# Attention backward on one core: V's fourth head is loaded as 120 rows and 8 rows, in two transfers

## The chip, the core and the metric

The kernel runs on one NeuronCore of a Trainium2 chip. The metric is device microseconds (us) of one execution. The kernel before was run three times: 698.41, 701.58 and 702.56 us, so its median is 701.58 us. The profile is of a further execution, which took 698.71 us.

## The reference

The kernel computes grouped-query softmax attention and all its gradients, in bfloat16. There are 32 batches, 32 query heads of 4 positions, 4 key/value heads of 2048 positions, and a head dimension of 128.

```python
k = jnp.repeat(k, 8, axis=1); v = jnp.repeat(v, 8, axis=1)     # 4 heads -> 32
scores = jnp.einsum("bhqd,bhkd->bhqk", q, k) * D ** -0.5
out = jnp.einsum("bhqk,bhkd->bhqd", softmax(scores), v)
dq, dk, dv = vjp(grad_out)                                     # four outputs: out, dq, dk, dv
```

K and V are read once (2 MB of each per batch), dK and dV are written once (2 MB of each per batch); q, grad_out, out and dq are small beside them (32 KB each per batch). So each batch moves a little over 8 MB between HBM and the on-chip memory SBUF.

## The kernel before

The work goes batch by batch. One batch has 128 query rows in all (32 heads x 4 positions), which fill the 128 partitions. A key/value head of 2048 positions lies in SBUF as 128 partitions (p) x 16 positions (c) x 128 elements, so that one partition's piece of one head is 4096 contiguous bytes in HBM.

For each batch the kernel loads K (`LK`, line 154, one transfer of 128 rows x 4096 bytes for each of four heads) and V (`LV`, line 160, likewise four). TensorE turns K and V, eight blocks of 128x128 at a time (`turned`, L181), and VectorE copies each result out of PSUM (L183). Then come scores (L198), maximum (L211), exponential on ScalarE (L222), the turned probabilities (L248, L250), the output `O` (L264, L274), the gradients of V (`dV`, L303 on TensorE, copied by ScalarE at L307), the gradient of the scores (`dP`, L338), its turned form, dQ (L264, L288) and dK (again L303 and L307). GpSimd scales the small operands of dV and dK (L231, in `NRM`).

What sets the order is a list of steps written out by hand, one list for the first batches (`HEAD`), one for the steady state (`STEADY`), one for the last (`TAIL`). Every engine executes its instructions in that order. In the steady state the loads of a batch (`LK+2 LV+2`) stand two batches ahead of the rest of the work, and the transposes of K and V one batch ahead.

Two queues issue transfers. SyncE (SP) issues all loads of K and V, in the order k0 k1 k2 k3 v0 v1 v2 v3 for each batch (the digit is the head). GpSimd (POOL) issues everything else: the stores of dV and dK (L326, two of 1 MB each per batch and gradient), of out (L276) and dq (L290), and once in four batches a load of q and grad_out (L142). Both queues feed the same 16 DMA engines. In the trace every transfer writes its completion semaphore 16 times, once for each DMA engine, so the time at which each of the 16 was done can be read, though not which engine it was. A 4096-byte row is one packet, and a load of 128 rows puts eight packets on each engine.

Three limits decide when a transfer can be issued:

- Its buffer must be free. K has three buffers (`kp`), V two (`vp`), the gradients on their way out four (`outp`), which is two batches of dV and dK.
- Its completion semaphore must be free. Each queue has eight of them (100 to 105, 107 and 109 for SP) and takes them in turn, so a transfer waits until the one that was issued eight before it on the same queue has landed.
- A queue issues in order, so a transfer that waits holds up all behind it.

Of the kernel before, what the change touches and what calls it, by code (L numbers as in the profile page):

```python
# [81 lines left out]
def kernel(ctx: ExitStack, tc: tile.TileContext, q, k, v, grad_out, out_0, out_1, out_2, out_3):  # L82
    nc = tc.nc
    B, Hq, Sq, D = q.shape
    NH, Sk = k.shape[1], k.shape[2]
    P = 128
# [41 lines left out]
    v_v = v.rearrange("b h (p c) d -> b h p (c d)", c=C)  # L128
# [27 lines left out]
    def LV(b):  # L156
        S = st[b]
        S["v"] = v_pool.tile([P, NH, C, D], BF16, name="v_sb")
        for h in range(NH):
            nc.sync.dma_start(out=S["v"][:, h].rearrange("p c d -> p (c d)"), in_=v_v[b, h])  # L160

    def bank16():

# [170 lines left out]
    def dP(b, i):  # L334
# [6 lines left out]
        banks.give(t)  # L341

    table = {"LK": LK, "LV": LV, "QDT": QDT, "O": O, "dQ": dQ, "NRM": NRM}
    for i, c in enumerate("ab"):
        for n, f in (("S", S_), ("EX", EX), ("dP", dP), ("ET", ET), ("dST", dST)):
# [16 lines left out]
    with tc.manual_schedule():  # L362

        for w in HEAD.split():
            w, b = w.split("@")
# [5 lines left out]
        for w in TAIL.split():  # L371
            w, b = w.split("@")
# [31 lines left out]
```

## Time and profile before

| | |
|---|---|
| profiled execution | 698.71 us, of which 696.7 us lie between the first and the last instruction (the span) |
| granted TensorE clock | 0.980 over the span |
| PE (TensorE) busy | 626.0 us, 90% of the span |
| DVE (VectorE) busy | 584.5 us, 84% |
| ACT (ScalarE) busy | 569.1 us, 82% |
| POOL (GpSimd) busy | 302.7 us, 43% |
| moved by DMA | 274.44 MB, mean 394 GB/s |
| issue to landing, median | k 13.8 us, v 18.6 us, dv 23.6 us, dk 22.1 us |

The page gives for each engine how long it was busy, then the span in 40 equal slices, in which a digit is the busy share in tenths. The DMA row is the mean over 16 engines. "Landing" is the last of the 16 completions of a transfer. The chain of waits is followed back from the last instruction: at each step to whatever released it. A line like "DMA out_dram<-dk" in it means that the time went by between the issue of that transfer and its landing, while something waited for it.

### The profile page before, as it was taken

To read this page: it belongs to the slowest core of one execution; us is meant where nothing else is said; L and a number is where in the kernel's file an instruction comes from. 1 tells how busy PE (TensorE), PEld (TensorE's weight loads), DVE (VectorE), ACT (ScalarE), POOL (GpSimd) and SP (SyncE) were. 2 spreads that over 40 slices of the span, in tenths; PEclk is the share of its full clock that TensorE was granted. 3 is DMA by queue.
4 is the path that set the end of the run, shared out by engine and by line. 5 is a ranking of instruction groups with operands and counts; after the bars stand their busy time and mean duration, and the time that the engine had idled before them with its cause. 6 is when DMAs were issued, how large, how long until landed. Compare 5 with 4: busy or idle time off the path is not lost.

```text
span 696.7 us, 28064 instructions
## 1 busy us (share of the span) xinstructions
PE 626.0 (90%) x12352; PEld 454.1 (65%) x12352; DVE 584.5 (84%) x992; ACT 569.1 (82%) x673; POOL 302.7 (43%) x506
## 2 busy tenths in 40 slices
PE   5899999999998989979999798998998889998982
PEld 4577776677676656666666676667766677666661
DVE  5999999999997998869988688888988869898960
ACT  0698989899887989869888687887888868888994
POOL 1355443555454435443354424544434543345452
PEclk9999999999999999999999899999999989999997
DMA  9989999999999999999999999999999999999767
GB/s 339 400 317 411 417 415 416 416 413 415 417 415 417 414 417 416 417 409 412 415 415 413 373 397 398 400 410 382 416 416 417 415 340 393 415 414 415 289 257 274
DMA packets 75577, 274.44 MB, mean 394 GB/s; under 512 B 8448, under 2 KB 8448, under 8 KB 75456
## 3 DMA queue, kind: packets, MB, share of 16 engines
q0 software_dynamic: 37536, 138.16, 49.3%
q1 hardware_dynamic: 37920, 134.50, 48.9%
q8 instruction: 96, 1.57, 0.8%
q14 instruction: 25, 0.20, 0.1%
HBM read 136.31 MB, written 136.31 MB: 391 GB/s over the span
## 4 chain that ended last, share of the span: by engine, by line
PE 43%; DMA 33%; ACT 6%; DVE 5%; POOL 5%; issue 5%; SPq 0%; POOLq 0%; DVEq 0%; ACTq 0%
PE banks L181 18%; DMA k_sb<-in_k_dram 15%; DMA out_dram<-dk 12%; PE banks L303 10%; PE banks L264 7%; ACT dv L307 5%; PE banks L248 5%; DMA out_dram<-dv 4%; PE banks L198 3%; POOL dop L231 2%; DMA v_sb<-in_v_dram 2%; DVE kt L183 2%; DVE ds L338 1%; ACT dk L307 1%; POOL qp L231 1%
## 5 line engine op out<-in xcount | busy, mean ns | idle before, releaser
L307 ACT CAST dv<-banks 128x1024 bf16<-128x1024 f32 x256 | 245.5, 1028 | 56.9 <-PE banks L303 56.3
L307 ACT CAST dk<-banks 128x1024 bf16<-128x1024 f32 x256 | 250.7, 1025 | 34.5 <-PE banks L303 23.6
L183 DVE COPY kt<-banks 128x1024 bf16<-128x1024 bf16 x256 | 164.3, 680 | 8.3 <-PE banks L181 8.3
L183 DVE COPY vt<-banks 128x1024 bf16<-128x1024 bf16 x256 | 166.2, 680 | 1.3 <-PE banks L181 0.9
L181 PE MATMUL banks<-ident,k_sb 128*128 128x128 bf16 x2048 | 145.8, 221 | 13.1 <-DMA k_sb<-in_k_dram 8.6
L181 PE MATMUL banks<-ident,v_sb 128*128 128x128 bf16 x2048 | 143.5, 220 | 14.3 <-ACT dv L307 9.7
L231 POOL TENSOR_SCALAR dop<-do_sb,rinv 32x128 bf16<-32x128 bf16 x128 | 76.7, 599 | 181.3 <-PE banks L303 118.9
L181 PEld LDWEIGHTS <-k_sb 128*128 128x128 bf16 x2048 | 120.8, 99 | 41.9 <-issue 31.7
L181 PEld LDWEIGHTS <-v_sb 128*128 128x128 bf16 x2048 | 122.2, 98 | 28.7 <-issue 23.3
L303 PE MATMUL banks<-dop,e 64*128 64x256 bf16 x1024 | 99.3, 276 | 15.1 <-POOL dop L231 11.3
L326 POOL DMA_DIRECT2D out_dram<-dv x62 | 43.7, 709 | 138.0 <-ACT dv L307 67.6
L338 DVE SCALAR_TENSOR_TENSOR ds<-banks,delta,e 128x1024 bf16<-128x1024 f32 x64 | 82.2, 1284 | 17.3 <-PE banks L198 14.3
L303 PE MATMUL banks<-qp,ds 64*128 64x256 bf16 x1024 | 86.4, 272 | 2.1 <-ACT dk L307 1.4
L231 POOL TENSOR_SCALAR qp<-q_sb,srinv 32x128 bf16<-32x128 bf16 x128 | 78.1, 610 | 10.7
L222 ACT ACTIVATE e<-banks,negb 128x1024 bf16<-128x1024 f32 x64 | 70.7, 1111 | 8.6 <-DVE negb L214 8.5
L211 DVE TENSOR_REDUCE m<-banks 128x1 f32<-128x1024 f32 x64 | 75.1, 1215 | 0.9 <-PE banks L198 0.9
L303 PEld LDWEIGHTS <-e 64*128 64x128 bf16 x1024 | 34.0, 94 | 63.1 <-issue 46.7
L250 DVE COPY et<-banks 128x1024 bf16<-128x1024 bf16 x64 | 41.3, 686 | 29.6 <-PE banks L248 29.6
L303 PEld LDWEIGHTS <-ds 64*128 64x128 bf16 x1024 | 42.2, 94 | 28.8 <-ACT dv L307 13.1
L326 POOL DMA_DIRECT2D out_dram<-dk x62 | 44.0, 713 | 13.6 <-DMA out_dram<-dk 13.0
L250 DVE COPY dst<-banks 128x1024 bf16<-128x1024 bf16 x64 | 43.5, 681 | 5.5 <-PE banks L248 3.6
L248 PE MATMUL banks<-ident,ds 128*128 128x128 bf16 x512 | 39.4, 221 | 7.1 <-ACT dk L307 6.8
(39 smaller groups left out, 484.1 us busy)
## 6 DMA issues: line engine op xcount, KB each, us to landing
k_sb<-in_k_dram SPq DMA_DIRECT2D x128, 512.0 KB, 13.8
v_sb<-in_v_dram SPq DMA_DIRECT2D x128, 512.0 KB, 18.6
out_dram<-dv POOLq DMA_DIRECT2D x64, 1024.0 KB, 23.6
out_dram<-dk POOLq DMA_DIRECT2D x64, 1024.0 KB, 22.1
out_dram<-o_sb POOLq DMA_DIRECT2D x32, 32.0 KB, 23.2
out_dram<-dq_sb POOLq DMA_DIRECT2D x32, 32.0 KB, 16.2
q_sb<-in_q_dram POOLq DMA_DIRECT2D x7, 128.0 KB, 21.9
do_sb<-in_grad_out_dram POOLq DMA_DIRECT2D x7, 128.0 KB, 22.0
```

What stands on the lines that cost most here:

```text
L181: nc.tensor.transpose(out=ps[:, 4 * hh + j, :], in_=S[which][:, 2 * (i % 2) + hh, 4 * (i // 2) + j, :], identity=ident[:])
L183: nc.vector.tensor_copy(out=S[f"{which}t{i}"][:], in_=ps)
L211: nc.vector.reduce_max(out=S["m"][:, i:i + 1], in_=S[f"s{i}"][1], axis=AX.X)
L222: nc.scalar.activation(out=S[f"e{i}"][:], in_=ps, func=ACT.Exp, bias=S["negb"][:], scale=scale, accum_out=S["l"][:, i:i + 1],)
L231: nc.gpsimd.tensor_scalar(out=t[r, h % 2, :], in0=src[r, :], scalar1=by[r, :], scalar2=None, op0=ALU.mult)
L248: nc.tensor.transpose(out=ps[:, u, :], in_=S[f"{src}{i}"][:, P * u:P * u + P], identity=ident[:])
L250: nc.vector.tensor_copy(out=S[f"{name}{i}"][:], in_=ps)
L264: nc.tensor.matmul(ps[G * h:G * h + G, :], lhsT=S[f"{xt}{c // 8}"][:, c % 8, G * h:G * h + G], rhs=S[kv][:, h, c, :], start=(c == 0), stop ...
L303: nc.tensor.matmul(ps[:, a, :, c, :], lhsT=S[f"{x}{i // 4}"][r, u:u + P], rhs=S[y][r, :, :], start=True, stop=True, tile_position=(2 * G * ...
L307: copy(out=S[name][:, :, 2 * i:2 * i + 2, :].rearrange("p h c d -> p h (c d)"), in_=banks.ap(t).rearrange("p a (j w) -> p (a j) w", j=2),)
L326: store.dma_start(out=dst[b][:, 2 * a:2 * a + 2, :], in_=o[:, 2 * a:2 * a + 2].rearrange("p h c d -> p h (c d)"))
L338: nc.vector.scalar_tensor_tensor(out=S[f"ds{i}"][:], in0=ps, scalar=S["delta"][:], in1=S[f"e{i}"][:], op0=ALU.subtract, op1=ALU.mult,)
```

## The change

The loads of V's heads 0 to 2 stay as they are. The load of head 3 becomes two transfers on the same queue: rows 0 to 119 (480 KB), then rows 120 to 127 (32 KB). They write the same bytes of the same buffer.

```diff
         for h in range(NH):
-            nc.sync.dma_start(out=S["v"][:, h].rearrange("p c d -> p (c d)"), in_=v_v[b, h])
+
+            for r in (slice(0, 120), slice(120, P)) if h == NH - 1 else (slice(0, P),):
+                nc.sync.dma_start(out=S["v"][r, h].rearrange("p c d -> p (c d)"), in_=v_v[b, h, r])
```

In the program built from it SP has 32 more transfers, one for each batch, and TensorE 32 more waits on a semaphore, because a reader of V's fourth head waits for both transfers. Nothing else moves: TensorE, VectorE, ScalarE and GpSimd execute the same instructions in the same order. The eight completion semaphores of the queue are still taken in turn, now by nine transfers for each batch. So each transfer waits on a different one than before: the third head of V on the 120 rows of the batch before, the 120 rows on the 8 rows of the batch before, and the 8 rows on the first head of K of their own batch.

## The prediction

> **What bounds the kernel now.** I read the DMA rows first: the page's slices and queues, then the busy time by stage (after the colon-marked stage and its length: TensorE, its weight loads, VectorE, ScalarE, GpSimd, then clock, DMA share and GB/s). DMA is full from 4 to 650 us; TensorE has some 8% to spare after 180 us.
>
> ```profile
> DMA  9989999999999999999999999999999999999767
> ...
> q8 instruction: 96, 1.57, 0.8%
> ```
> ```profile
> 60.00:180.00 120.00, 117.22 (x2366) 85.56 (x2355) 110.31 (x190) 108.33 (x130) 56.62 (x94) 1.00 1.03 415
> 180.00:380.00 200.00, 183.61 (x3656) 131.66 (x3657) 172.99 (x293) 168.20 (x199) 91.19 (x151) 0.99 1.03 414
> 380.00:640.00 260.00, 237.53 (x4642) 172.09 (x4636) 219.61 (x374) 213.63 (x254) 113.20 (x186) 0.97 1.01 400
> ```
>
> Until 180 us TensorE is busy 117.22 of 120 us and batches follow each other every 19.5 us (in the chain of waits the copies of dv come at 128.43, 147.92 and 167.44 us). From 180 us on the chain of waits is made of transfers: first loads of K, once per batch and 21.1 us apart, later stores waited for by ScalarE because all four output buffers are out.
>
> ```profile
> 199.11 16.95 DMA k_sb<-in_k_dram
> ...
> 220.24 16.81 DMA k_sb<-in_k_dram
> ...
> 241.24 17.01 DMA k_sb<-in_k_dram
> ...
> 615.44 27.13 DMA out_dram<-dk
> 642.67 1.02 ACT dk L307
> ```
>
> A transfer ends with the last of its 16 engines. I took the 16 completion times of each transfer from the trace; medians from issue, us:
>
> | stage | transfers | 1st | 8th | 15th | 16th |
> |---|---|---|---|---|---|
> | 60–180 | loads | 9.6 | 11.7 | 12.9 | 14.6 |
> | 180–380 | loads | 6.9 | 12.8 | 14.6 | 19.9 |
> | 380–640 | loads | 5.5 | 6.6 | 8.4 | 15.1 |
> | 380–640 | stores of dk, dv | 8.9 | 9.3 | 10.8 | 23.9 |
>
> So **one engine is late in every transfer**: the store issued at 615.44 us was done on 15 engines at 627.98 us and on the sixteenth at 642.57 us. For each place in the order I subtracted from the time the work done by then (155.4 ns per 4096-byte packet, the distance from start to start on a busy engine; 80 ns per 2048-byte packet; 6 ns per semaphore write). What is left, at 80, 380 and 640 us: the first 11.4, 13.2, 30.4 us; the eighth to fifteenth about 12.7, 20.8, 32; **the sixteenth 12.7, 28.3, 44.3**. The last loses 31.6 us in 560 us, 5.64%, and never rests: in the trace its packets run alone from 653.9 to 657.2 us. Followed packet by packet back from 655 to 460 us they take 167.8 ns on average, where the median of all packets is 159. The middle eight lose 8.1 us from 80 to 380 us, 2.7%; the 96 instruction packets of queue q8, each of which I see delay one engine by about 1.27 us, would cost eight engines 15.2 us each over the run, 2.6%. After 380 us the fifteen wait for the one: their own losses of 11 us more are idle time, in bursts.
>
> **The change, part by part.**
>
> *What an engine has to do.* Per batch: 128 packets x 155.4 = 19.89 us, plus two 2048-byte packets, one packet of q or grad_out and some 14.5 semaphore writes, 0.40: **20.29 us**. With its loss the late engine needs 20.29 / (1 - 0.0564) = **21.50 us**, a middle one 20.29 / (1 - 0.027) = 20.85.
>
> *The 120 rows.* How they spread the trace doesn't show. The nearest row is the 128-row load with eight packets on each of 16 engines. Bounds: each engine keeps eight rows, so fifteen engines work and one has none (15 x 8 = 120); or all sixteen still take part with seven or eight, and none is relieved. I take the first, since it is the existing division with one share missing. The missing share is the last in order; I take the late engine to be at the end, since in stores of the tail (issued at 657.26 us) the other fifteen completed at even steps of 13 to 20 ns with no hole before the last, where a late engine in the middle would leave one. That is a weak sign, and the first rival is built on it. Relief: 8 x 163.8 (167.8 less 4 overlap) = 1.31 us per batch, which leaves the late engine at 20.19 us.
>
> *The 8 rows.* Bounds: one packet more on eight engines (+0.16 us with the semaphore write) or eight on one (+1.25 us). I take one packet each, by the same row, where each engine has an equal share, and put them on the middle eight, the worse place: 20.85 + 0.16 = **21.01 us**. That is then the slowest engine.
>
> The Trainium skill (DMA: Bandwidth & Descriptors, "Why a DMA increments its semaphore by 16 and not by 1") says the number of engines is the largest divisor of the row count up to 16, the lowest-numbered ones on this queue: fifteen for 120, eight for 8. By that rule, which no run here shows yet, the sum is the one taken.
>
> *The issue.* 32 more issues on SP at 0.33 to 0.47 us, in a queue that stands waiting for buffers and landings:
>
> ```profile
> SPq L154 <- PE banks L303: 293.5, 29, 13.4
> SPq L160 <- PE banks L303: 80.2, 27, 5.1
> SPq L160 <- DMA v_sb<-in_v_dram: 72.3, 46, 2.5
> ...
> SPq L154 <- DMA k_sb<-in_k_dram: 52.0, 33, 2.4
> ```
>
> Cost nothing: 293.5 us of waiting for buffers cover 32 x 0.47 = 15 us. Without that cover it would be 0.5 us per batch.
>
> *The waits.* Nine transfers share eight semaphores, so v2 and the 120 rows wait for a landing one transfer later than now, and the 8 rows for k0 of their own batch; behind them in SP stand the next batch's four K loads. k0 has landed 13.8 us after its issue (median), while v3 is issued some 12 us after k0: about 2 us later than now, and k0 of the next batch comes 9 us after that. Of loads in flight seven large ones are left, 56 packets per engine, and with the stores taking turns 56 x 2 x 155 ns = 17.4 us of queue, still full. I take zero; the bounds are a gain of nothing and the third rival's loss. TensorE's extra wait per batch: a semaphore wait of 17 ns on SP and POOL, 32 x 17 ns = 0.5 us, left out.
>
> *Sum.* 21.50 - 21.01 = 0.49 us per batch. From 180 to 657 us the DMA sets the pace: 477 / 21.5 = 22.2 batches, **10.9 us**. Taking off 1.4 us for pauses that don't come from the late engine (TensorE waits 4.1 us for "issue" at 389 and 562 us, and the DMA runs dry around them) leaves 9.5. The tail after 657 us has 39 us in which the DMA isn't full; I leave it as it is. What is late next are the middle eight engines. 698.71 - 9.5 = 689.2 us against the profiled execution. The median of the runs stands 2.9 us above that execution, so the same gain gives 692.1 there; midway between the two I predict **690.5**. Something under 1%, 7 us, is what a measurement of this kernel can tell from no change.
>
> **The rivals.**
>
> *Another engine is the late one.* Then it isn't relieved, and if it is among the eight it gets a row more: 21.50 + 0.16 us over 22.2 batches, +3.6 us, up to 32 x 0.16 = +5.2: 702 to 707. For: no view gives the engine's number. Against: the even steps above. The Trainium skill (same page, "Latency and other measured facts") calls engines 7 and 15 usually slower, and guesses that descriptors of the GpSimd queue are the cause. The trace agrees in part: in the opening, with loads alone, eight loads in a row end with the same 0.80 us between the fifteenth and sixteenth engine, so nobody is slow; the drift comes with the stores. It shows one such engine, not two. If it is 7, this rival holds.
>
> *The rows don't divide as taken* (the change doesn't do what it says): all sixteen engines keep a part of the 120 rows. Then nothing is relieved: 698.7 to 704, within 1%. The Trainium skill (same page, "Rules for kernel authors") says against such splits that both parts share the same engines, so one transfer of 128 rows is best; by that the late engine would have to keep its share, this same time. The 16 completions speak against equal engines.
>
> *Relief, but little of it reaches the end.* Stores and loads both come earlier, yet the compute between them (19.5 us per batch, TensorE 90% busy) is close behind 21.01, and its stalls leave engines dry. A third of the gain, 3 us: 696 to 699.
>
> *Slower: the ninth transfer.* With nine transfers on eight semaphores the period can't be shorter than 9/8 of the time from issue to landing. Now that time is up to 21 us for V's loads with a factor of 8/8. If landing doesn't fall below 18.7 us the ninth transfer binds; at 19.6, half the way from 20.9, the period is 22.05 us, +0.55 x 22.2 = **+12 us**, 711 to 714. For: 72.3 and 52.0 us of waiting for such landings already. Against: 15 of 16 engines land at 14.6 and 8.4 us, and a shorter queue lands sooner.
>
> **How the numbers follow.** Forecast 0.58 (684 to 694.5; the midpoint of execution and median is 700.1, the low end is all 32 x 0.49 = 15.7 us off it, the high end is 7 us off the median), little of it 0.14, another engine 0.10, rows not divided 0.06, ninth transfer 0.12. Part of the forecast's low edge falls within 1%, about 0.02. So faster 0.56, same 0.32, slower 0.12. The range reaches over the rivals within 1%, 684 to 706, and leaves out the ninth transfer and the edges.
>
> **What would show it.** Right: the sixteenth completion of loads and stores comes within 2 to 4 us of the fifteenth; the median landing of dk and dv falls from 22 to under 16 us; the stores of 26 us leave the chain of waits; GB/s after 380 us rises from 400 towards 410. Wrong: the gap between the last two stays (another engine, or rows not divided), or V's loads wait on SP for landings far over 72 us (ninth transfer), or packets of the 120-row load take much more than 159 ns.

## The result, and the profile after

The changed kernel took **709.21 us** (median of four, 708.56 to 710.22); the kernel before 701.88 us (median of four: the three runs named above and 702.17). The ratio is **1.0116, 95% interval 1.0091 to 1.0141**: slower, where 690.5 us was predicted. The profiled execution took 710.22 us, with a span of 708.3 us, against 698.71 and 696.7 us before.

From the page of the kernel before, the count of packets and the chain that ended last by line:

```profile
DMA packets 75577, 274.44 MB, mean 394 GB/s; under 512 B 8448, under 2 KB 8448, under 8 KB 75456
...
PE banks L181 18%; DMA k_sb<-in_k_dram 15%; DMA out_dram<-dk 12%; PE banks L303 10%; PE banks L264 7%; ACT dv L307 5%; PE banks L248 5%; DMA out_dram<-dv 4%; PE banks L198 3%; POOL dop L231 2%; DMA v_sb<-in_v_dram 2%; DVE kt L183 2%; DVE ds L338 1%; ACT dk L307 1%; POOL qp L231 1%
```

From the page of the changed kernel, the DMA slices, the rate in the same 40 slices, the count of packets, and the chain that ended last by engine and by line:

```profile
DMA  9999999999999999999999999999999999999767
GB/s 294 347 364 392 415 415 415 412 407 411 413 413 409 409 410 410 398 397 409 410 402 400 380 390 403 402 387 387 413 405 400 394 398 395 389 388 394 302 245 275
DMA packets 75802, 274.45 MB, mean 387 GB/s; under 512 B 8672, under 2 KB 8672, under 8 KB 75680
...
DMA 57%; PE 32%; ACT 3%; issue 3%; DVE 2%; SPq 1%; POOL 1%; POOLq 0%; DVEq 0%; ACTq 0%
DMA k_sb<-in_k_dram 51%; PE banks L183 14%; PE banks L305 8%; PE banks L266 6%; DMA v_sb<-in_v_dram 5%; ACT dv L309 3%; PE banks L250 2%; PE banks L200 1%; DVE ds L340 1%; DVE kt L185 1%; ACT dk L309 1%; DVE vt L185 1%; SPq L154 0%; DVE m L213 0%; PE banks L173 0%
```

The DMA is as full as before and moves less: 387 GB/s where it was 394. Loads of K are 51% of the chain, where before they were 15% and stores of dk 12%. And the count of packets tells the division: those under 512 bytes, the semaphore writes among them, rose from 8448 to 8672, by 224 = 32 x 7. So the fourth head's load writes 23 completions per batch in place of 16: fifteen for the 120 rows and eight for the 8 rows. The Trainium skill's rule (DMA: Bandwidth & Descriptors, "Why a DMA increments its semaphore by 16 and not by 1"), by which the row count's largest divisor up to 16 gives the number of engines, agrees with this trace.

Busy time by stage after (columns as in the prediction: stage, length, then TensorE, its weight loads, VectorE, ScalarE, GpSimd, clock, DMA share, GB/s):

```profile
60.00:180.00 120.00, 114.88 (x2306) 83.19 (x2302) 108.84 (x185) 106.24 (x125) 55.60 (x92) 1.00 1.03 412
180.00:380.00 200.00, 180.74 (x3618) 131.14 (x3616) 170.73 (x291) 165.29 (x197) 85.46 (x142) 0.99 1.02 407
380.00:640.00 260.00, 233.12 (x4616) 167.82 (x4614) 220.10 (x372) 212.45 (x253) 112.54 (x186) 0.99 1.02 395
```

Every stage lost some rate: 415 to 412, 414 to 407, 400 to 395 GB/s. TensorE's clock was no worse (0.99 to 1.00), so it isn't the clock.

The chain of waits of the changed kernel between 400 and 520 us (start, length, what) shows one load of K per batch, 21.7 us apart, and no store:

```profile
422.50 17.50 DMA k_sb<-in_k_dram
...
444.21 17.57 DMA k_sb<-in_k_dram
...
465.99 17.13 DMA k_sb<-in_k_dram
...
487.33 17.47 DMA k_sb<-in_k_dram
```

What SP's queue waited for, in the changed kernel (total us, times, longest; L154 issues K, L162 V, and L305 is before's L303):

```profile
SPq L162 <- DMA v_sb<-in_v_dram: 168.1, 84, 2.8
SPq L154 <- PE banks L305: 163.7, 29, 12.3
SPq L154 <- DMA k_sb<-in_k_dram: 72.9, 45, 2.5
...
SPq L154 <- DMA v_sb<-in_v_dram: 44.6, 23, 2.4
SPq L162 <- DMA k_sb<-in_k_dram: 36.6, 28, 2.4
SPq L162 <- PE banks L305: 25.3, 10, 4.0
```

SP now stands 322 us waiting for landings (the four DMA lines), where the two shown of before gave 124; for buffers 189 us, where it was 374.

The completions of each transfer, read as in the prediction (medians from issue, us):

| stage | transfer | 1st | last but one | last |
|---|---|---|---|---|
| 180–380 | 128-row loads | 4.8 | 12.7 | 18.8 |
| 180–380 | 8 rows, on eight engines | 6.3 | 12.7 | 19.1 |
| 380–640 | 128-row loads | 4.8 | 7.5 | 18.8 |
| 380–640 | 120 rows, on fifteen engines | 8.0 | 10.7 | 21.2 |
| 380–640 | **8 rows, on eight engines** | 6.3 | 8.2 | **19.0** |
| 380–640 | stores of dk, dv | 8.2 | 11.6 | 20.3 |

This answers the main question before any experiment: **the late engine is one of the eight that take the 8 rows**. One engine was relieved: at 380 to 640 us the first completion of whole loads now stands 0.8 us ahead of the second (4.8 and 5.6 us), where that distance was 0.2 us. It was not the late one. That one got a row more.

Where the time came from, by the landing of the first K transfer of a batch: the eleventh batch's at 192.3 us before and 198.3 after (+6.0); from there to the last batch 21.20 us per batch before and 21.72 after (21 batches, +11.0); from the last batch's K to the last completion 57.0 us before and 51.5 after (-5.5). Together +11.5 us between the two profiled executions, of which 3.2 us is that before's profiled one lay below its median of 701.88, and 1.0 us that the changed one's lay above its own.

### The profile page after: what moved, and what is told of

The parts are those of the page before. It is cut to its first block, busy times and chain, and to the rows that moved or that the text cites. A ratio compares the mean times of both kernels' runs of the same rounds, so it can differ in the third digit from the quotient of the medians.

```text
span 708.3 us, 28128 instructions
## 1 busy us (share of the span) xinstructions
PE 626.5 (88%) x12352; PEld 453.3 (64%) x12352; DVE 587.8 (83%) x992; ACT 569.3 (80%) x673; POOL 301.9 (43%) x506
## 2 busy tenths in 40 slices
DMA packets 75802, 274.45 MB, mean 387 GB/s; under 512 B 8672, under 2 KB 8672, under 8 KB 75680
## 3 DMA queue, kind: packets, MB, share of 16 engines
q1 hardware_dynamic: 38144, 134.50, 49.3%
q0 software_dynamic: 37536, 138.16, 49.3%
## 4 chain that ended last, share of the span: by engine, by line
DMA 57%; PE 32%; ACT 3%; issue 3%; DVE 2%; SPq 1%; POOL 1%; POOLq 0%; DVEq 0%; ACTq 0%
DMA k_sb<-in_k_dram 51%; PE banks L183 14%; PE banks L305 8%; PE banks L266 6%; DMA v_sb<-in_v_dram 5%; ACT dv L309 3%; PE banks L250 2%; PE banks L200 1%; DVE ds L340 1%; DVE kt L185 1%; ACT dk L309 1%; DVE vt L185 1%; SPq L154 0%; DVE m L213 0%; PE banks L173 0%
## 5 line engine op out<-in xcount | busy, mean ns | idle before, releaser
L185 DVE COPY kt<-banks 128x1024 bf16<-128x1024 bf16 x256 | 166.2, 684 | 21.4 <-PE banks L183 20.8
L183 PE MATMUL banks<-ident,k_sb 128*128 128x128 bf16 x2048 | 152.0, 225 | 32.0 <-DMA k_sb<-in_k_dram 25.3
L183 PEld LDWEIGHTS <-k_sb 128*128 128x128 bf16 x2048 | 123.8, 101 | 63.2 <-issue 33.6
L305 PE MATMUL banks<-dop,e 64*128 64x256 bf16 x1024 | 97.2, 273 | 5.9 <-ACT dv L309 1.9
L305 PE MATMUL banks<-qp,ds 64*128 64x256 bf16 x1024 | 86.4, 274 | 3.1 <-ACT dk L309 1.4
L233 POOL TENSOR_SCALAR qp<-q_sb,srinv 32x128 bf16<-32x128 bf16 x128 | 77.4, 605 | 10.7
L305 PEld LDWEIGHTS <-e 64*128 64x128 bf16 x1024 | 33.7, 94 | 52.5 <-issue 35.3
L305 PEld LDWEIGHTS <-ds 64*128 64x128 bf16 x1024 | 41.0, 94 | 30.8 <-ACT dv L309 13.2
L200 PE MATMUL banks<-vt,qdt 128*32 128x512 bf16 x512 | 40.7, 384 | 2.8 <-issue 2.6
## 6 DMA issues: line engine op xcount, KB each, us to landing
out_dram<-dv POOLq DMA_DIRECT2D x64, 1024.0 KB, 21.8
out_dram<-dk POOLq DMA_DIRECT2D x64, 1024.0 KB, 17.3
out_dram<-dq_sb POOLq DMA_DIRECT2D x32, 32.0 KB, 11.6
```

Of the source, the lines that this page charges most:

```text
L183: nc.tensor.transpose(out=ps[:, 4 * hh + j, :], in_=S[which][:, 2 * (i % 2) + hh, 4 * (i // 2) + j, :], identity=ident[:])
L185: nc.vector.tensor_copy(out=S[f"{which}t{i}"][:], in_=ps)
L200: nc.tensor.matmul(ps[G * h:G * h + G, a, :], lhsT=S["qdt"][:, col, G * h:G * h + G], rhs=xt[:, 4 * (h % 2):4 * (h % 2) + 4, :].rearrange( ...
L233: nc.gpsimd.tensor_scalar(out=t[r, h % 2, :], in0=src[r, :], scalar1=by[r, :], scalar2=None, op0=ALU.mult)
L305: nc.tensor.matmul(ps[:, a, :, c, :], lhsT=S[f"{x}{i // 4}"][r, u:u + P], rhs=S[y][r, :, :], start=True, stop=True, tile_position=(2 * G * ...
```

## The experiments

In the diffs "-" is the changed kernel where only its row slices differ, and the kernel before elsewhere. "Row more" is what the fifth engine gets per batch; that it is the fifth comes out of the second group.

| run | split of the fourth head | row more | transfers on SP | ratio to before, 95% |
|---|---|---|---|---|
| e1 | V 120, 8 | 1 | 9 | 1.0121 (1.0097–1.0146) |
| e2 | V 112, 16 | 0 | 9 | 1.0009 (0.9992–1.0026) |
| e3 | V 120 alone | 0 | 8 | 1.0025 (1.0012–1.0038) |
| e4 | V 120, 7, 1 | 1 | 10 | 1.0109 (1.0089–1.0128) |
| e5 | V 120, 5, 3 | 1 | 10 | 1.0145 (1.0114–1.0176) |
| e6 | V 120, 8 from the fourth batch | 1 | 9 | 1.0116 (1.0083–1.0149) |
| e7 | V and K 120, 8 | 2 | 10 | 1.0375 (1.0343–1.0407) |
| e9 | V 120, 3, 3, 2 | 0 | 11 | 1.0048 (1.0031–1.0066) |
| e16 | V and K 112, 16 | 0 | 10 | 1.0180 (1.0145–1.0214) |
| e18 | V 120, 4, 4 | 0 | 10 | 1.0054 (1.0026–1.0082) |

### The transfer, the relief, the row

e1 is the changed kernel once more: 709.62 us.

> The changed kernel once more, as the yardstick for the others of this chip. Theory 1 (the late DMA engine is one of the eight that carry the 8 rows: it has one packet more per batch, about 0.17 us x 32 = 5.4 us) and theory 2 (nine transfers take turns on eight completion semaphores, so loads are issued later) both expect what was measured, 1.0116 of before, some 8 us.

e2 keeps two transfers, but both lie on all sixteen engines:

```diff
-            for r in (slice(0, 120), slice(120, P)) if h == NH - 1 else (slice(0, P),):
+            for r in (slice(0, 112), slice(112, P)) if h == NH - 1 else (slice(0, P),):
```

> V's fourth head as 112 rows and 16 rows. Both divide by 16, so every engine keeps its eight rows (7 + 1); what stays of the change is the ninth transfer per batch and one semaphore write more per engine (32 x 6 ns = 0.2 us). Theory 1: the time of before, 702 us, within 1 us, and the gap between the 15th and 16th completion of the loads as before. Theory 2: the whole loss, 709 us. If both share it, in between.

701.85 us, no difference. What SP's queue waited for in this kernel looks like the changed one all the same:

```profile
SPq L161 <- DMA v_sb<-in_v_dram: 168.1, 86, 2.7
SPq L154 <- PE banks L304: 152.9, 29, 11.8
SPq L154 <- DMA k_sb<-in_k_dram: 74.7, 49, 2.5
...
SPq L154 <- DMA v_sb<-in_v_dram: 47.7, 25, 2.5
SPq L161 <- DMA k_sb<-in_k_dram: 42.0, 28, 3.0
```

332 us of waiting for landings, at no cost. So the ninth transfer as such isn't the cause, and the rise of this wait, which the prediction had named as a sign of it, is no sign.

e3 loads the 120 rows and, from the third batch on, not the 8 (V stays in two fixed buffers, whose last rows are of an earlier batch):

```diff
-            nc.sync.dma_start(out=S["v"][:, h].rearrange("p c d -> p (c d)"), in_=v_v[b, h])
+            r = slice(0, 120) if h == NH - 1 and b >= 2 else slice(0, P)
+            nc.sync.dma_start(out=S["v"][r, h].rearrange("p c d -> p (c d)"), in_=v_v[b, h, r])
```

> The 8 rows are not loaded from the third batch on (the two buffers of V are fixed and keep old rows there, so part of V's fourth head is left out): eight transfers per batch, and no engine has more packets than before. Theory 1: 702 us or up to 1 us less, since the late engine keeps its eight rows of this load. Theory 2: 702 us as well. A third theory, that a load spread over 15 engines is slow in itself (packets over 159 ns), expects 705 us or more.

703.05 us: relieving the sixteenth engine of a whole share gains nothing, and is even 1.8 us slower. So the prediction's relief was of an engine that didn't matter, and the 8 rows are what costs the larger part.

### Which engine

e4, e5 and e18 divide the 8 rows so that fewer engines share each piece. The count of packets under 512 bytes is 8672 in e18 too, that is 15 + 4 + 4 completions.

```diff
-            for r in (slice(0, 120), slice(120, P)) if h == NH - 1 else (slice(0, P),):
+            for r in (slice(0, 120), slice(120, 127), slice(127, P)) if h == NH - 1 else (slice(0, P),):   # e4
+            for r in (slice(0, 120), slice(120, 125), slice(125, P)) if h == NH - 1 else (slice(0, P),):   # e5
+            for r in (slice(0, 120), slice(120, 124), slice(124, P)) if h == NH - 1 else (slice(0, P),):   # e18
```

> 120 rows, 7 rows and 1 row. If a transfer runs on the largest number of engines up to 16 that divides its rows, beginning at the first, these are engines 0 to 14, 0 to 6, and 0. Theory 1 with the late engine being number 7: the 7-row transfer has no late completion (last within 3 us of the one before), and the late engine has what it had before, 702 us plus what the tenth transfer costs. Theory 1 with the late engine among 0 to 6: the 7-row transfer ends 6 to 10 us late like the 8-row one, 709 us or more. Theory 2: two transfers more instead of one, 7 us each, 716 us.

> V's fourth head as 120, 5 and 3 rows: by the division seen so far the 5 rows lie on the first five engines, the 3 rows on the first three. Theory A (one late engine, among the first seven but not the first, gets one row more and pays for it): the completions tell its place, and the time goes with the rows it gets. If it is the second or third, both small transfers end with a gap of 6 us or more in the stage 180 to 380 us, and the time is 714 to 718 us (two rows more). If it is the fourth or fifth, only the 5 rows do, and the time stays at 708 to 710 us. If it is the sixth or seventh, neither does, no row more falls on it, and the time is 701 to 704 us. Theory B (the loads of fewer than 128 rows are slow in themselves, whoever is late: in the opening their packets took some 300 ns in place of 159): 708 to 711 us whatever the place.

> V's fourth head as 120, 4 and 4 rows; the 4 rows lie on the first four engines. If the late engine is the fourth, it gets two rows more and both small transfers end late: twice the price of one, 714 us or more. If it is the fifth, it gets none, the small transfers end with no gap, and the time is 702 to 706 us as with 3, 3 and 2 rows.

Medians at 380 to 640 us, from issue: e4's 7 rows end at 9.5 and, the last, 18.6 us; its single row at under 7 us. e5's 5 rows end at 9.5 and 18.7 us, its 3 rows at 7.4 and 7.6. e18's 4 rows end at 9.4 and 10.2. If each piece lies on the first engines in order, as the Trainium skill's section named above has it for this queue, the late one is among the first five and not among the first four: **the fifth**. The times follow it: 708.90 and 711.08 us with a row on it, 703.74 without. The probes ran on four chips (e4, e5, e9 and e18 each on its own). Putting them together takes the late engine to be the same one on each; e4 alone says no more than the second to the seventh, e5 alone the fourth or the fifth. None of them speaks for another engine.

### One row, two rows, ten transfers

e9 cuts the 8 rows so that the late engine gets none, at the price of eleven transfers; e6 leaves the first three batches whole; e7 splits K's fourth head too; e16 does the same with 112 and 16 rows.

```diff
-            for r in (slice(0, 120), slice(120, P)) if h == NH - 1 else (slice(0, P),):
+            for r in (slice(0, 120), slice(120, 123), slice(123, 126), slice(126, P)) if h == NH - 1 else (slice(0, P),):   # e9
+            for r in (slice(0, 120), slice(120, P)) if h == NH - 1 and b >= 3 else (slice(0, P),):   # e6
+            for r in (slice(0, 120), slice(120, P)) if h == NH - 1 else (slice(0, P),):   # e7, in LK as in LV
+            for r in (slice(0, 112), slice(112, P)) if h == NH - 1 else (slice(0, P),):   # e16, in LK as in LV
```

> V's fourth head as 120, 3, 3 and 2 rows: eleven transfers per batch in place of nine, but by the run with 5 and 3 rows the late engine (the fourth or fifth) is in none of the small ones and keeps its eight rows, as before the change. If what costs the time is the row more on the late engine: 5.2 us less than the change, what is left is the 120 rows' own cost (1.8 us where they were loaded alone), so 701 to 705 us. If it is the number of transfers on eight semaphores, with landings of 19 us: 11/9 of the change's period where these waits bind, 715 us or more. If the small loads are slow in themselves wherever they lie: 708 to 712 us.

> The change (120 and 8 rows) from the fourth batch on, the first three batches as before. In the changed kernel the load of the fourth batch's K is issued at 42.8 to 43.7 us in place of 40.9, after an opening in which packets of the 120 and 8 rows took 280 to 360 ns where 159 is usual. If that delay of 2 to 3 us is carried to the end: 706 to 707.5 us. If the late engine alone decides, which is idle at times in the opening: 709 us as with the whole change.

> K's fourth head is also loaded as 120 and 8 rows: the late engine gets two rows more per batch, the relieved one loses sixteen. If each row more costs what the first did (8 us with its slow opening): 716 to 719 us. If only the late engine's 0.17 us per row counts on top of a cost that comes once: 713 to 715 us. If the cost was that of a ninth transfer on eight semaphores, the tenth adds as much again or more, but then the 112 and 16 rows would have cost it too.

> K's and V's fourth heads both as 112 and 16 rows: ten transfers per batch on SP's eight semaphores as in the run that took 727 us, but every engine keeps its rows. If the price there was the rows on the late engine: 700 to 706 us. If it was ten transfers that land late on eight semaphores: 715 us or more.

e9 took 704.60 us: with two transfers more than the change, and the same packets, it is 5 us faster, because the fifth engine keeps its rows. Against the mean of e1, e4 and e6 (1.0115), e9 and e18 (mean 1.0051) put **the price of the one row at 0.64%, 4.5 us**; with e5 (1.0145) in that mean it is 0.72%, 5.0 us. 32 x 0.1614 us, a packet and its semaphore write, is 5.2 us. In return e9's pieces put three rows more on each of the first two engines, and at 180 to 380 us they end late: at 11.9 and then 16.3 us with three rows, at 8.6 and 13.3 with two. So one of these two engines falls behind as well, which may be part of what e9 still costs.

e6 shows no saving (1.0116). In the opening of e1 packets took 213 to 356 ns (medians of each us) while partial loads were under way; e6 has whole loads there and is no faster. That doesn't rule the opening out: e6's interval is 0.33% wide to either side, 2.3 us, and its fourth batch's K was issued at 42.3 us, hardly before e1's 42.8, so it took little of the named delay away. e2, with slow partial loads in its opening too, issued it at 40.6 us, as before did (40.9). What the opening costs stays open.

e7 took 727.27 us, 26 us over before and far more than two rows. e16 has ten large transfers too and no row more, and took 713.89 us, between the two outcomes put on record: 13.7 us over before by the medians, 12.6 by the ratio, and 13 us less than e7, where two rows are 10.3 us of work. In e16 SP stands 442 us waiting for landings, where e2 has 332. That fits the mechanism of the "slower" rival, if it begins at the tenth transfer that ends on the late engine and not at the ninth; e9's small pieces, which don't touch that engine and land after 8.6 to 11.1 us at 380 to 640 us, give their semaphores back early. It isn't shown to be that: e16 also splits K's fourth head, which e2 leaves whole, and no run separates the two.

### What makes the engine late, and does it set the pace

e8 issues the stores of dv and dk from ScalarE; e10 the same, with K and V loaded two heads to a transfer; e11 only loads in pairs; e12 loads in pairs and stores from SP; e13 is e12 with the stores issued later in the list.

```diff
-                store.dma_start(out=dst[b][:, 2 * a:2 * a + 2, :], ...)
+                nc.scalar.dma_start(out=dst[b][:, 2 * a:2 * a + 2, :], ...)     # e8, e10; nc.sync in e12
...
-        for h in range(NH):
-            nc.sync.dma_start(out=S["k"][:, h].rearrange("p c d -> p (c d)"), in_=k_v[b, h])
+        for a in range(0, NH, 2):     # e10 to e13, K and V
+            nc.sync.dma_start(out=S["k"][:, a:a + 2].rearrange("p h c d -> p h (c d)"), in_=k_v[b, a:a + 2].rearrange("h p x -> p h x"))
...
+        flush("dv")     # e13, at the start of NRM: SP's stores of a finished dv
+            flush("dk")     # e13, in dV 4, which stands behind the next loads
```

> V whole as before; the stores of dv and dk are issued by ScalarE in place of GpSimd, 128 issues. If the late engine is late because the large stores come from the GpSimd queue, the gap between the fifteenth and sixteenth completion (5.4 us at 180 to 380, 6.5 us for loads and 13.4 us for stores at 380 to 640 us) falls to under 2 us, and the DMA moves more per us in the later stages; by the middle engines' 20.85 us per batch the time could be 687 to 695 us, unless the 128 issues on ScalarE (some 0.4 us each, 51 us, on 569 us of work) hold its copies up: then 700 to 715 us with the gap gone. If one engine is late whatever the queue, the gap stays and the time is 700 us or more.

> Stores of dv and dk from ScalarE's queue, and K and V loaded two heads to a transfer (1 MB each). With the stores there the late engine was gone (gap 0.3 to 0.5 us) and the time was lost in loads that waited for semaphores last used by stores of dk (263 us of SP's waits). Eight transfers per batch on eight semaphores now: each waits for the one of its own place a batch ago, which has landed 10 us after its issue. If the late engine set the pace of the kernel before: gap under 1 us and 675 to 695 us. If it didn't, or if ScalarE's issues hold its copies up: 700 us or more with the gap gone.

> K and V loaded two heads to a transfer, stores on GpSimd as before: the control for the run beside it. Four transfers of loads per batch on SP's eight semaphores, so no load waits for a landing; the late engine keeps its work (same packets). If it sets the pace: within 1% of before, 697 to 707 us, the gap of 5 us and more still there. If semaphore waits of the loads cost the kernel before something: faster than 694 us.

> Stores of dv and dk issued by SP, K and V loaded two heads to a transfer: eight transfers per batch on SP's eight semaphores, and ScalarE issues nothing (its issues of 0.75 to 1.57 us stood in the chain of waits of the run with ScalarE's queue, which was 4.4% slower though no engine was late). If the late engine comes with the large stores from GpSimd and sets the pace of the kernel before: gap under 2 us, 675 to 695 us. If SP's order holds loads up behind stores (a store waits for its copies on ScalarE): the gap is gone, SP's waits move to its stores, and the time is 700 us or more. If the late engine is late on any queue that stores 4 MB per batch beside the loads: the gap of 5 us or more is back and the time is about 700 us.

> As the run before (stores of dv and dk on SP, K and V two heads to a transfer), but SP's stores stand later in the list: those of dv in the next batch's NRM, those of dk behind the next loads, when their copies are done, so that SP doesn't stand waiting for ScalarE (442 us there) with loads behind it. If the late engine sets the pace of the kernel before: gap under 2 us, the pace falls towards TensorE's 19.5 us per batch of the stage before 180 us or the other engines' 20.3 to 20.9, and the time is 665 to 692 us. If something else holds the kernel at 700 us: 697 us or more with the gap gone.

e8 took 742.14 us, e10 732.86 and e12 751.47. In all three no engine was far behind: from 180 us on the fifteenth and sixteenth completion are 0.3 (loads) and 0.5 us (stores) apart in e8, and at most 1.6 us in e10 and e12. In each another wait had taken over, and the DMA moved less (e8 370 GB/s, before 394). In e8 loads of K wait for landings of dk, with which they have nothing in common but a completion semaphore, so the two queues share these. The first line is the longest of SP's waits in e8, the others its DMA issues (last column: us to landing):

```profile
SPq L154 <- DMA out_dram<-dk: 263.2, 28, 11.1
```
```profile
k_sb<-in_k_dram SPq DMA_DIRECT2D x128, 512.0 KB, 6.5
v_sb<-in_v_dram SPq DMA_DIRECT2D x128, 512.0 KB, 10.4
out_dram<-dv ACTq DMA_DIRECT2D x64, 1024.0 KB, 10.3
out_dram<-dk ACTq DMA_DIRECT2D x64, 1024.0 KB, 11.9
```

In e10 the chain that ended last has hardly a transfer left; ScalarE's copies and issues are in it:

```profile
PE 49%; ACT 34%; ACTq 8%; issue 5%; DVE 2%; DMA 1%; POOL 0%; SPq 0%; DVEq 0%; POOLq 0%
```

In e12 SP stands waiting for ScalarE, with loads behind it:

```profile
SPq L326 <- ACT dk L307: 441.9, 37, 17.2
```

I took this as a sign that GpSimd's queue makes the engine late. **e13 refutes it**, and neither outcome put on record for e13 had the gap back. There SP issues all loads and all stores of dv and dk, and its stores wait 148 us for ScalarE, where e12's waited 461. It took 701.35 us (1.0007, 0.9995 to 1.0019), as before, and the late engine is back: gaps of 6.8 and 7.4 us at 180 to 380 us, 9.0 and 9.3 us at 380 to 640 us, for loads and stores. From e13's page, the chain that ended last and the DMA issues:

```profile
DMA 60%; PE 29%; ACT 5%; DVE 4%; issue 1%; POOL 0%; ACTq 0%; SPq 0%; DVEq 0%; POOLq 0%
...
k_sb<-in_k_dram SPq DMA_DIRECT2D x64, 1024.0 KB, 17.3
v_sb<-in_v_dram SPq DMA_DIRECT2D x64, 1024.0 KB, 17.2
out_dram<-dv SPq DMA_DIRECT2D x64, 1024.0 KB, 19.4
out_dram<-dk SPq DMA_DIRECT2D x64, 1024.0 KB, 18.9
```

So one engine is slower with the large stores on GpSimd's queue and on SP's. I read e8, e10 and e12 so that its delay grows only where it gets no pause and other waits left it time to catch up there; for ScalarE's queue, which only e8 and e10 use, no run without such waits shows it. Two kernels with different queues, orders and sizes of transfer, the one before and e13, end at the same time, with that engine late in both. e11 fits: 699.68 us (0.9989, 0.9977 to 1.0001), stores ending at 10.7 and 23.9 us at 380 to 640 us.

An account of the late engine over each profiled execution, with the prediction's prices for a packet and a semaphore write (time of the last completion, less the work given to the late engine):

| | before | changed | e3 | e18 | e13 | e4 | e6 | e7 |
|---|---|---|---|---|---|---|---|---|
| work, us | 647.5 | 652.7 | 647.5 | 647.5 | 646.8 | 652.7 | 652.2 | 657.9 |
| not used, us | 46.9 | 53.2 | 49.3 | 51.5 | 51.1 | 51.4 | 52.7 | 65.7 |
| last completion, us | 694.4 | 705.9 | 696.9 | 699.1 | 697.9 | 704.1 | 704.9 | 723.6 |

The changed kernel's engine has 5.2 us more of work and 6.3 us more not used. About 4 us of these 6.3 are that the two profiled executions lay on opposite sides of their medians, so the table is no measure of what the split costs beside the row.

### The split in the kernel with all large stores on SP

e14 is e13 with V in three transfers (two heads, one, one); e15 splits its last one into 120 and 8 rows; e17 does so with V's heads 0 to 2 in one transfer, to have nine transfers as e14 has.

```diff
+        for h, r in ((2, slice(0, P)), (3, slice(0, P))):     # e14, behind one transfer of V's heads 0 and 1
+        for h, r in ((2, slice(0, P)), (3, slice(0, 120)), (3, slice(120, P))):     # e15
+        for r in (slice(0, 120), slice(120, P)):     # e17, of head 3, behind one transfer of heads 0 to 2
```

> The same with V as two heads, one head and one head, nine transfers per batch on eight semaphores: the control for the run beside it. The same time as with V in two transfers, within 1%, if landings of 12 us or less leave the semaphores free in time.

> The same as the control with V's fourth head as 120 and 8 rows. If the split costs only because of the late engine: within 0.4% of the control (under 3 us), since no engine is late here. If the loads of fewer than 128 rows cost in themselves or the added transfer does: 5 us or more above the control.

> The kernel with all large stores on SP and V's fourth head as 120 and 8 rows, now with V's heads 0 to 2 in one transfer: nine transfers per batch, as many as in the control of 701.9 us, and the late engine has its row more. If the 35 us were the tenth transfer: 707 to 713 us, the row's price as in the change. If they are the split's own: 725 us or more.

e14 took 701.86 us, e15 736.71 (1.0520, 1.0480 to 1.0560) and e17 737.76 (1.0513, 1.0478 to 1.0548). Here the same split costs 36 us, and not by the tenth transfer. Busy time by stage of e17 shows the rate at 384 GB/s, where e14 had 408 and 399 in the same stages:

```profile
180.00:380.00 200.00, 177.99 (x3452) 129.61 (x3446) 164.10 (x278) 157.74 (x189) 57.86 (x102) 0.96 1.01 384
380.00:640.00 260.00, 229.77 (x4424) 166.25 (x4420) 214.90 (x360) 206.06 (x245) 73.23 (x129) 0.97 1.01 384
```

Three engines are late there in place of one: whole loads at 380 to 640 us complete at 5.5 us on the first engine, 9.7 on the thirteenth, and 14.6, 16.3 and 18.1 on the last three (e14: 7.6, 7.8, 8.3, 17.2 for the last four). The 8 rows end by 5.3 on six engines and at 14.0 and 16.1 on two. What makes two more engines late isn't settled.

The packets show where most of the time goes. Of the 4096-byte packets of SP's queue at 180 to 640 us, 1.9% took over 200 ns in e14, 8.4% in e15 and 7.9% in e17. Most of these long packets in e15 and e17 (68% and 58%) stand within 2 us of the eighth completion of the transfer ahead of the 120 rows, that is, about when the 120 rows begin; these stretches are 17% of the time. In them 74.8 (e15) and 78.3 (e17) packets start per us, outside them 94.4 and 94.5. That is 0.83 and 0.69 us of 4 lost per batch, by this estimate 27 and 22 of the 36 us. So the other outcome named for e15 fits: the partial loads cost in themselves here, where all large transfers go through one queue. In the changed kernel, where GpSimd's stores go on beside them, 10.8% of SP's packets are slow in the same stretches and 2.3% outside, but as many start (47.0 and 47.8 per us). No run tests this by itself.

My expectation for e15, that the split costs under 3 us, rested on the late engine being gone, which e13, run beside it, refuted; and the row's price doesn't explain 36 us.

## Why the prediction was wrong

**What bounds the kernel: right.** One engine late in every transfer, which sets the pace from 180 us on. It is the fifth, and it is as late, and the time the same 701 us, with the stores on another queue and the loads in other sizes (e13). A row more on it costs 4.5 to 5.0 us, near the 5.2 us of work that it is. One reading beside the sum is off: the 15.2 us of queue q8 are 2.2% of the span of 696.7 us, not 2.6%.

***The 120 rows*: this step failed.** That they go as eight rows on fifteen engines was right. That the late engine is the one left out was wrong: "I take the late engine to be at the end", on the even steps of one store's other fifteen completions. e3 leaves the sixteenth engine out without the 8 rows and is 0.25% slower. The 1.31 us per batch were never to be had. The weak sign misled because completions are read in order of time: the place in the order in which engines end says nothing of the engine's place in the division.

***The 8 rows*: the count was right, the place wrong.** One packet on each of eight engines, as taken; but put on "the middle eight, the worse place", where the worst place was on the late engine itself. The sum then is the first rival's: 21.50 + 0.16 = 21.66 us per batch. The K landings of the changed kernel came 21.72 us apart, but that the two lie so close is luck: those of before came 21.20 apart, not 21.50.

**The rival *another engine is the late one* held**, with +3.6 to +5.2 us against the row's 4.5 to 5.0. Its total of 702 to 707 us was too low by what else the split costs: e9 and e18, which give the fifth engine no row, are 3.4 to 3.8 us slower than before. About 1.8 us of it is there with the 120 rows alone (e3). Where this comes from isn't settled; a ninth transfer as such isn't it (e2), and the share of the opening is open (e6). The Trainium skill (DMA: Bandwidth & Descriptors, "Latency and other measured facts") names engines 7 and 15 as usually slower, and guesses at GpSimd's descriptors. The runs show neither: counted from one the engine is the fifth, and it is as late in e13, where GpSimd issues only the small transfers.

***The waits*: zero was right for the ninth transfer** (e2: 0.65 us, interval -0.6 to 1.8), and the rival that priced it at 12 us is refuted for nine. With ten transfers such a price was seen (e16: 12.6 to 13.7 us), but with K's split in it.

***The issue*: covered as taken.** e9 issues 96 transfers more than before and e18 64 more, and both stay within 3.8 us.

**The sum**: 22.2 batches x 0.49 us of gain had the wrong sign. The pace of 21.50 us is what the account of the late engine gives (20.29 / (1 - 0.0548) = 21.47). Between the eleventh and the last batch the K landings lost 21 x 0.52 us, but this is not the loss in time: in e2 they came 21.45 us apart, and from the last of them to the end it was 52.5 us in place of 57.0, at the time of before.

**The signs.** One that was named as right came true although the theory was wrong: the stores of 26 and 27 us left the chain of waits. Another came half true: dk's landing fell from 22.1 to 17.3 us, dv's only to 21.8. Both only tell that the loads became the later ones. Of the signs named as wrong, slow packets around the 120 rows came in part (10.8% over 200 ns there), but e2 has 7.2% there and lost nothing. The sign that told was the gap of the last two completions, which stayed: 10.6 us for loads at 380 to 640 us.

## What to carry to other kernels

When the DMA is full, ask which single engine ends last and what each transfer puts on it; a mean over engines hides both. A load that isn't a multiple of 16 rows changes the division, and taking work from one engine helps only if it is shown, by a small transfer that includes or excludes it, that this is the late one. Pieces of 8, 7, 5, 4 or 3 rows are such a probe, and their completions in one profile would have told it before the change was made.

## What the runs showed of the hardware

- One DMA engine, the fifth by these probes, loses 5.5 to 5.8% of its time from 180 to 640 us (the slope of the account above: 0.0548 before, 0.0565 changed, 0.0577 in e13) while loads and stores run without pause, with the large stores on GpSimd's queue or on SP's. In e8, where other waits give it pauses, the gaps are 0.3 to 0.5 us.
- Stores on ScalarE's queue took semaphores from the same eight as SP's loads: SP waited 263 us for landings of dk in e8.
- Packets of partial loads are slow where no other queue's large transfers are beside them: in the opening of e1, while the 120 and 8 rows were under way (13 to 17 us), packets took 213 to 316 ns (medians of each us) where whole loads have 159; with 112 and 16 rows (e2) 248 to 322. With all large transfers on SP's queue 40% (e15) and 31% (e17) of the packets around the 120 rows took over 200 ns, in the changed kernel 11%.
- With all large transfers on one queue the split made two further engines late and cost 36 us (e15, e17). The packets put 22 to 27 us of it, an estimate, on the partial loads.
- No kernel here is faster than the one before by more than its interval; the nearest is e11, loads in pairs, at 0.9989.
